# Splitting the first key load, loading one sketch matrix through GpSimd, and a new issue order in a polysketch attention and rational feed-forward kernel

## The chip, the cores and the metric

The kernel runs on one core of a Trainium2 chip. The metric is the device time of one execution in microseconds (us); lower is better.

## The reference

Linear attention with a polynomial sketch, then a feed-forward layer with a rational activation. Four batches, four heads, 1088 positions, head size 32; 4352 tokens of width 128 and a hidden width of 2048 in the second part.

```
def phi(x):                       # S1, S2: 8 x 32
    a = einsum('rd,bhsd->bhsr', S1, x)
    b = einsum('rd,bhsd->bhsr', S2, x)
    return einsum('bhsi,bhsj->bhsij', a, b)      # 64 features
q_p, k_p = phi(q), phi(k)
kv  = einsum('bhsf,bhsd->bhfd', k_p, v);  z = sum(k_p, axis=2)
num = einsum('bhsf,bhfd->bhsd', q_p, kv); den = einsum('bhsf,bhf->bhs', q_p, z) + 1e-6
x   = (num / den) as 4352 x 128
h   = x @ w_in                                    # 128 x 2048
P   = a0 + a1 h + a2 h^2 + a3 h^3
Q   = 1 + |b0| |h| + |b1| h^2
out = (P / (Q + 1e-6)) @ w_out                    # 2048 x 128
```

## The kernel before, in words

The kernel is one list of steps (976 before the change). Each step belongs to one engine and issues one or a few instructions. The schedule is written out: the table `PLACE` gives each step its position, and `run` emits the steps in that order, so every engine and every DMA queue works strictly in the order of the table. A step that has to wait holds back all that stands behind it on its engine. `ON_ACT` lists which of the steps that could run on either ScalarE (ACT) or VectorE (DVE) go to ACT. `FILLS` puts idle matmuls on TensorE (PE) in front of some places, which keep that engine running at the start. The numbers in `step` and `dma` calls (cost, rate, slack, early, land) are those of the planner that made the table; they put nothing into the program.

The work has two parts that are interleaved:

- **Attention.** `keys` handles one batch's keys: DVE transposes the key tile in 32x32 blocks into `kT` (L415, L417), PE multiplies with the sketch matrix S12 (L435), ACT copies one half of the sketches out of PSUM (`b_sk`, L440), DVE multiplies the halves to features (`k_p`, L443), PE multiplies features and values (L454), ACT keeps the result (`kvz`, L471). For the first batch ("wide") this goes in five parts. `queries` does the same for queries: transposes (L496), sketches (L518 in the "direct" form, L546 in the "spread" form, which sends the sketches through DRAM and back with DMAs), features (L530, L533, L554), products with `kvz` (L586), a division on DVE (guard L595, inverse L599, quotient L602), a transpose back on PE (L608) and a copy into `xT` on ACT (L615).
- **Feed-forward.** 29 units of up to 3072 columns each: hidden matmuls on PE (L688), evacuation on ACT (L692), |h| on DVE (L703), the denominator (L708 or L710, L713), 1/Q as exp(-ln Q) on ACT (L716, L719), polynomial products on DVE (L728, L731, L734, L746, L749), output matmuls on PE (L784), a transpose on DVE (L796) and the store. `w_in` is loaded in two halves of 1024 columns; `w_out` is loaded in two halves (called wo0 and wo1 here) and made into five scaled bf16 copies, ten steps of 128x1024 (y0f0 to y4f1; L391, L393 on ACT, L395 on DVE).

At the start nothing can be computed until data is in. S1 and S2 (1 KB each) go to the two halves of one small tile `s_raw`; DVE copies it to `s_rep` (L352, its first instruction), PE transposes that with the identity `ident` made by GpSimd (L349), and DVE makes the sketch matrices S12 and SAB from it (L355, L362). Batch 0's keys (`k0`, 128 x 4352 bytes) are loaded by ACT's DMA queue; S1, S2, the first 256 columns of the queries (`q0_a`), the values (two DMAs), the rest of the queries (`q0_b`), and the weights come by SP's queue. All DMA issues are ordinary waiting instructions of their queue.

Of the kernel before, what the change touches and what calls it, by code (L numbers as in the profile page):

```python
# [20 lines left out]
def kernel(  # L21
# [103 lines left out]
    def d_four(n, ptr):  # L125
# [88 lines left out]
    )  # L214
    ON_ACT = (
        24, 26, 28, 29, 31, 32, 328, 351, 379, 454, 478, 502, 535, 612, 636, 669, 688, 693, 744, 878, 889,
        914, 932, 946, 951, 953, 960,
    )
    FILLS = {5: 15, 14: 4, 66: 5, 70: 1}
# [46 lines left out]
    def dma(out_, in_, rank, mbytes, after=(), uses=(), eng=SP, early=0.0, rate=300, cost=0.46, slack=0.3, behind=None):  # L266
        def go():
            (nc.sync if eng == SP else nc.scalar).dma_start(out=out_() if callable(out_) else out_,
                                                            in_=in_() if callable(in_) else in_)
        return step(eng, cost, go, rank, after=after, uses=uses, land=mbytes * 1e3 / rate, early=early,  # L270
                    slack=slack, behind=behind)
# [19 lines left out]
    s_l.append(load_s(1, -205.9, SP, behind=s_l[0]))  # L291
    FIRST = 256
    k0_l = load_k(0, k0, -207, slack=0.0, rate=304, eng=ACTE)
    table = step(ACTE, 1.3, lambda: nc.scalar.preload_act_table_set("natural_log_exp_and_others"), -205, behind=k0_l[0])
    q0_a = dma(lambda: q0.t[:, 0:FIRST], flat(q, 0)[:, 0:FIRST], -203.8, 0.131, (), [q0], rate=250, slack=0.1, behind=s_l[1])
    v0_l = load_v(0, v0, -203.7, slack=0.25, rates=(180, 200), behind=q0_a)
    ab_in = []
    for c, w, x in ((4, 2, moe_b), (0, 4, moe_a)):
        ab_in.append(dma(ab_row[:, c:c + w], bass.AP(tensor=x.tensor, offset=x.offset, ap=[[w, 1], [1, w]]), -203.6, 0.001,
                         eng=ACTE, cost=0.45, slack=1.0, behind=ab_in[0] if ab_in else k0_l[0]))  # L300
    w_l = [None] * 2

    def load_w(x, rank):
        c = x * 1024
        w_l[x] = dma(w_in_sb[:, c:c + 1024], moe_w_in[:, c:c + 1024], rank, 0.524, early=LATER, rate=300, slack=0.4, behind=v0_l[1])

    load_w(0, -196)
    q0_b = dma(lambda: q0.t[:, FIRST:S], flat(q, 0)[:, FIRST:S], Q0B_RANK, 0.426, (), [q0], rate=200, slack=0.3, behind=q0_a)
    load_w(1, W1_RANK)
    k1 = Buf("kq")  # L310
    k1_l = load_k(1, k1, K1L_RANK, early=LATER, slack=0.2, behind=v0_l[1], rate=350)
# [551 lines left out]
```

## Time and profile before

| what | value |
|---|---|
| time, median of 3 runs | 266.96 us (266.92 to 267.07) |
| time of the profiled execution | 267.34 us |
| its span in the profile | 265.5 us (1.84 us lie around it) |
| granted TensorE clock, mean | 0.996 |
| DVE waits for `s_raw` before its first instruction | 4.5 us |
| data moved by DMA | 20.13 MB, mean 76 GB/s |

The profile has times from the start of the span. "Idle before" is time in which an engine stood still in front of an instruction, with what released it. SPq is SP's DMA queue. Because each engine keeps its order, a row that starts later moves all rows behind it on its engine, unless there is idle time to take it up.

### The profile page before, as it was taken

How to read it: one execution, taken by the hardware profiler on the slowest of the kernel's cores; microseconds unless marked ns; L12 is line 12 of the kernel's file. 1: busy time of each engine (PE TensorE's matmuls, PEld its weight loads, DVE VectorE, ACT ScalarE, POOL GpSimd, SP SyncE). 2: the span in 40 equal slices, each digit the busy share in tenths (PEclk: the TensorE clock that was granted, in tenths of full speed). 3: DMA queues.
4: the chain of work that ended last, by engine and by line, in shares of the span. 5: the costliest groups of instructions: out<-in, count | busy, mean ns of one | idle time of the engine just before them, and what ended most of it. 6: DMA issues, size and time to landing. Idle time of an engine off the chain costs nothing.

```text
span 265.5 us, 4239 instructions
## 1 busy us (share of the span) xinstructions
PE 257.2 (97%) x1663; PEld 140.4 (53%) x1663; DVE 252.7 (95%) x293; ACT 248.4 (94%) x209; POOL 2.7 (1%) x25
## 2 busy tenths in 40 slices
PE   7999999999999999999999999999999999999994
PEld 5767645644544464344445555444444476565682
DVE  3989899999999999999999999999999999999994
ACT  2499999999999999999999999999999999999991
POOL 4000000000000000000000000000000000000000
PEclk9999999999999999999999999999999999999998
DMA  7948344620556503035001522200002002010032
GB/s 202 331 151 223 121 127 118 159 61 0 145 131 168 164 2 108 13 79 131 28 6 44 150 65 46 41 0 0 0 10 32 0 0 40 4 29 11 0 52 40
DMA packets 29063, 20.13 MB, mean 76 GB/s; under 512 B 19316, under 2 KB 24948, under 8 KB 29044
## 3 DMA queue, kind: packets, MB, share of 16 engines
q1 hardware_dynamic: 28352, 19.24, 28.8%
q10 hardware_dynamic: 692, 0.62, 0.8%
q8 instruction: 13, 0.21, 0.4%
q14 instruction: 6, 0.05, 0.1%
HBM read 16.65 MB, written 3.21 MB: 75 GB/s over the span
## 4 chain that ended last, share of the span: by engine, by line
PE 35%; ACT 29%; DVE 21%; issue 8%; DMA 4%; SPq 1%; DVEq 0%; ACTq 0%
PE h_ps L688 21%; ACT t L692 7%; ACT ln L716 7%; ACT t L719 7%; PE out_ps L784 6%; ACT t L725 5%; DVE t L713 4%; DVE t L728 4%; DVE t L731 3%; DMA kq<-in_q_dram 3%; DVE t L749 2%; PE att_ps L586 2%; DVE t L703 2%; PE att_ps L546 2%; DVE t L708 2%
## 5 line engine op out<-in xcount | busy, mean ns | idle before, releaser
L688 PE MATMUL h_ps<-xT,w_in_sb 128*128 128x512 f32 (+1 forms) x320 | 128.0, 535 | 0.8 <-ACT xT L615 0.6
L784 PE MATMUL out_ps<-t,w_out 128*128 128x512 bf16 (+1 forms) x498 | 101.7, 346 | 0.6 <-DVE t L728 0.5
L688 PEld LDWEIGHTS h_ps<-xT,w_in_sb 128*128 128x128 f32 x320 | 58.6, 190 | 45.2 <-issue 33.8
L784 PEld LDWEIGHTS <-w_out 128*128 128x128 bf16 x498 | 47.4, 98 | 51.9 <-issue 21.1
L692 ACT CAST t<-h_ps 128x1024 bf16<-128x1024 f32 (+1 forms) x69 | 68.5, 1025 | 0.9 <-PE h_ps L688 0.9
L716 ACT ACTIVATE ln<-t 128x3072 f32<-128x3072 bf16 (+4 forms) x29 | 64.7, 2230 | 0.3 <-DVE t L713 0.2
L719 ACT ACTIVATE t<-ln 128x3072 bf16<-128x3072 f32 (+4 forms) x29 | 64.7, 2232 | 0.1
L713 DVE TENSOR_TENSOR t<-t,t 128x3072 bf16<-128x3072 bf16 (+4 forms) x29 | 40.4, 1392 | 0.6 <-ACT t L710 0.6
L728 DVE TENSOR_TENSOR t<-t,t 128x3072 bf16<-128x3072 bf16 (+4 forms) x29 | 40.4, 1394 | 0.0
L731 DVE TENSOR_TENSOR t<-t,t 128x3072 bf16<-128x3072 bf16 (+3 forms) x23 | 32.6, 1423 | 0.1
L725 ACT ACTIVATE t<-t,a_sb 128x3072 bf16<-128x3072 bf16 (+2 forms) x12 | 32.0, 2665 | 0.0
L703 DVE TENSOR_SCALAR t<-t 128x3072 uint16<-128x3072 uint16 (+4 forms) x29 | 22.5, 776 | 0.3 <-ACT t L692 0.2
L734 DVE TENSOR_TENSOR t<-t,t 128x3072 bf16<-128x3072 bf16 (+1 forms) x13 | 21.6, 1660 | 0.0
L708 DVE TENSOR_SCALAR t<-t,b_abs 128x3072 bf16<-128x3072 bf16 (+2 forms) x22 | 21.5, 975 | 0.1
L586 PEld LDWEIGHTS att_ps<-kvz,a_all 128*64 128x64 f32 x288 | 9.6, 137 | 6.8 <-issue 2.2
L586 PE MATMUL att_ps<-kvz,a_all 128*64 128x66 f32 x288 | 11.5, 226 | 0.6 <-DVE a_all L530 0.4
L749 DVE TENSOR_TENSOR t<-t,t 128x1024 bf16<-128x1024 bf16 (+3 forms) x10 | 11.2, 1124 | 0.1
L710 ACT ACTIVATE t<-t,b_abs 128x1024 bf16<-128x1024 bf16 (+4 forms) x7 | 11.3, 1611 | 0.0
L554 DVE TENSOR_TENSOR a_all<-a_all,b_all 128x768 f32<-128x768 f32 (+2 forms) x11 | 9.6, 869 | 0.0
L443 DVE TENSOR_TENSOR k_p<-att_ps,b_sk 128x768 f32<-128x768 f32 x9 | 8.4, 949 | 0.8 <-ACT b_sk L440 0.6
L454 PEld LDWEIGHTS att_ps<-v_sb,k_p 128*64 128x64 f32 x216 | 6.7, 138 | 2.3 <-issue 1.3
L746 DVE TENSOR_TENSOR t<-t,t 128x3072 bf16<-128x3072 bf16 (+3 forms) x6 | 7.7, 1276 | 0.0
(74 smaller groups left out, 143.8 us busy)
## 6 DMA issues: line engine op xcount, KB each, us to landing
a_all<-sk_d SPq DMA_DIRECT2D x6, 384.0 KB, 3.9
b_all<-sk_d SPq DMA_DIRECT2D x12, 192.0 KB
kq<-in_k_dram SPq DMA_DIRECT2D x3, 544.0 KB, 7.3
kq<-in_q_dram SPq DMA_DIRECT2D x3, 544.0 KB
a_all<-sk_d SPq DMA_DIRECT2D x4, 320.0 KB
b_all<-sk_d SPq DMA_DIRECT2D x8, 160.0 KB
v_sb<-in_v_dram SPq DMA_DIRECT2D x4, 288.0 KB, 4.9
v_sb<-in_v_dram SPq DMA_DIRECT2D x4, 256.0 KB, 4.3
```

The costliest lines, as they stand in the source:

```text
L586: nc.tensor.matmul(nd.t[x:x + 64, o:o + 2 * KW], lhsT=(av(c)[:, o0 + x:o0 + x + 64] if how == "direct" else q_p.t[:, c * n + o0 + x:c * n ...
L688: nc.tensor.matmul(h.t[:, cols[x] - cols[x0]:cols[x + 1] - cols[x0]], lhsT=w_in_sb[:, f * 128:(f + 1) * 128], rhs=xT[:, xpos(t0):xpos(t0) ...
L692: nc.scalar.copy(out=hh.t[:, cols[x0]:cols[x1]], in_=h.t[:, 0:cols[x1] - cols[x0]])
L703: nc.vector.tensor_scalar(out=u.t[:, :n].bitcast(U16), in0=hh.t[:, :n].bitcast(U16), scalar1=0x7FFF, scalar2=None, op0=AX.bitwise_and)
L708: nc.vector.tensor_scalar(out=w.t[:, :n], in0=u.t[:, :n], scalar1=ab1, scalar2=ab0, op0=AX.mult, op1=AX.add)
L713: nc.vector.tensor_mul(out=y.t[:, :n], in0=w.t[:, :n], in1=u.t[:, :n])
L716: nc.scalar.activation(out=ln.t[:, :n], in_=y.t[:, :n], func=ACT.Ln, bias=1.0 + 1e-6)
L719: nc.scalar.activation(out=r.t[:, :n], in_=ln.t[:, :n], func=ACT.Exp, scale=-1.0)
L725: nc.scalar.activation(out=p.t[:, :n], in_=hh.t[:, :n], func=ACT.Identity, scale=a3, bias=a2)
L728: nc.vector.tensor_mul(out=s.t[:, :n], in0=hh.t[:, :n], in1=r.t[:, :n])
L731: nc.vector.tensor_mul(out=(hh if mode == 3 else p).t[:, :n], in0=hh.t[:, :n], in1=s.t[:, :n])
L784: nc.tensor.matmul(o[0].t[:, :bl[x][1]], lhsT=w_sb[y_][:, bl[x][2], :], rhs=src.t[:, cols[x]:cols[x + 1]], start=(o[1] == 1), stop=(o[1] = ...
```

## The change

- Batch 0's keys are loaded in two DMAs, both on ACT's queue, one behind the other: the first half of the columns (2176 bytes of each of 128 partitions), then the second. The DVE transposes of the wide keys are cut to match: instead of two pieces that both read the whole tile (tiles 0 to 4, tiles 4 to 8 with the rest), there are three: tiles 0 to 8 of the first half (one instruction of 128x512), then tiles 0 to 4 and tiles 4 to 8 with the rest of the second half. The first sketches of keys wait for the first two pieces.
- S2 is loaded by a DMA of GpSimd, the first thing that GpSimd does in the kernel's body, ahead of its memsets. SP no longer issues S2.
- The memset of the tile `idle`, which the idle matmuls read, moves from GpSimd to DVE.
- `PLACE`, `FILLS` and the planner's numbers are new; the order of nearly all 978 steps is different. `ON_ACT` is the same for all units; of the ten `w_out` steps, y1f1 and y3f0 go from DVE to ACT and y0f0 and y1f0 from ACT to DVE.

The new table gives these orders at the start (the place of a step decides; K is the first batch's keys, p0 to p4 its five parts, Q1 the queries 0 to 256, Q2 256 to 512, Q3 512 to 768, Q4 the rest):

```
DVE before: s_rep, K tiles 0-4, S12, Q1 transpose, SAB x2, p0 features, K tiles 4-8 + rest, p1, p3, p2, Q1 features, p4,
            Q3/Q2/Q4 transposes, y4f1, Q1 guard/inverse/quotient, Q2 features, y1f1, Q2 division, y3f0, y0f1, next keys, unit 0
DVE after:  s_rep, K first half, S12, K second half 0-4, 4-8 + rest, SAB x2, Q1 transpose, p0, p1, p3, p2, Q1 features, p4,
            Q3/Q2/Q4 transposes, y0f1, Q1 guard/inverse/quotient, Q2 features, y1f0, Q2 division, next keys, y0f0, unit 0
ACT before: k0, moe_b, moe_a, table, p0, b_abs, a_sb, p1, p3, Q1, p2, p4 copies, kvz, Q3 copy, y2f1, Q2 copy, y3f1, Q1 xT,
            y2f0, y0f0, y1f0, unit 0 evacuation
ACT after:  k0 first, k0 second, moe_b, moe_a, table, p0, a_sb, p2, p1, b_abs, p3, Q1, p4 copies, y3f1, y2f1, kvz, Q3 copy,
            y3f0, Q2 copy, Q4 copy, Q1 xT, y1f1, y4f0, unit 0 evacuation
SP before:  S1, S2, q0_a, v0 low, v0 high, q0_b, wo1, wo0, w_in first half, next keys, ...
SP after:   S1, q0_a, v0 low, v0 high, wo1, q0_b, wo0, w_in first half, next keys, ...
```

The diff, with the tables cut:

```
 PLACE = (
-    0, 3, 1, 19, 6, 7, 8, 2, 18, 16, 9, 58, 55, 12, 10, 4, 5, 13, 24, 25, 49, 21, 23, 22, 83, 97, 84,
...
+    0, 1, 3, 4, 8, 9, 10, 11, 5, 6, 24, 16, 96, 25, 23, 12, 2, 13, 14, 20, 21, 15, 28, 29, 34, 108, 63,
...
-    24, 26, 28, 29, 31, 32, 328, ...
+    28, 29, 30, 31, 32, 33, 330, ...
-FILLS = {5: 15, 14: 4, 66: 5, 70: 1}
+FILLS = {13: 12, 18: 3, 74: 1, 79: 1}
...
-s_l.append(load_s(1, -205.9, SP, behind=s_l[0]))
+nc.gpsimd.dma_start(out=s_raw[R:2 * R], in_=S2)
+def go():
+    pass
+s_l.append(step(POOL, 0.65, go, -205.9, land=0.003, early=0.75, slack=0.4))
-k0_l = load_k(0, k0, -207, slack=0.0, rate=304, eng=ACTE)
+k0_l = []
+for m in range(2):
+    x = slice(m * S // 2, (m + 1) * S // 2)
+    k0_l.append(dma(lambda x=x: k0.t[:, x], flat(k, 0)[:, x], -207 + 0.1 * m, 0.279, (), [k0], rate=(460, 380)[m], slack=0.15,
+                    eng=ACTE, behind=k0_l[0] if m else None, name=("first", "go")[m]))
...
-nc.gpsimd.memset(idle, 0.0)
+nc.vector.memset(idle, 0.0)
...
+            if m is not None:
+                nc.vector.transpose(out=hT[:, m, :, t0:t1], in_=halves(kb.t, t0, t1)[:, m])
...
-    pieces = ((0, 4, (0, 1), False), (4, 8, (0, 1), True)) if wide else ((0, 8, (0,), False), (0, 8, (1,), True))
+    if wide:
+        pieces = ((0, 8, (), False, 0), (0, 4, (), False, 1), (4, 8, (), True, 1))
+        costs, loads = (0.6, 0.33, 0.33 + 0.15), (k_l[:1], k_l, k_l)
+    else:
+        pieces = ((0, 8, (0,), False), (0, 8, (1,), True))
...
-        sk = step(PE, 0.13 * n + 0.1, sketches, r - 0.2, after=(tr[:1] if wide and t1 <= 4 else tr) + s12, uses=[kT, ab],
+        sk = step(PE, 0.13 * n + 0.1, sketches, r - 0.2, after=(tr[:2] if wide and t1 <= 4 else tr) + s12, uses=[kT, ab],
```

More of the change, by code (lines that the diff above doesn't have):

```diff
@@ L165 @@
     PLACE = (
[48 rows of a table removed]
[48 rows of a table added]
     )
     ON_ACT = (
-        24, 26, 28, 29, 31, 32, 328, 351, 379, 454, 478, 502, 535, 612, 636, 669, 688, 693, 744, 878, 889,
-        914, 932, 946, 951, 953, 960,
+        28, 29, 30, 31, 32, 33, 330, 353, 381, 456, 480, 504, 537, 614, 638, 671, 690, 695, 746, 880, 891,
+        916, 934, 948, 953, 955, 962,
     )
-    FILLS = {5: 15, 14: 4, 66: 5, 70: 1}
+    FILLS = {13: 12, 18: 3, 74: 1, 79: 1}
     NW = 5 if '4' in MODES else 3
@@ L264, with dma @@
     k0, q0, v0 = Buf("kq"), Buf("kq"), Buf("v_sb")
-    def dma(out_, in_, rank, mbytes, after=(), uses=(), eng=SP, early=0.0, rate=300, cost=0.46, slack=0.3, behind=None):
+    def dma(out_, in_, rank, mbytes, after=(), uses=(), eng=SP, early=0.0, rate=300, cost=0.46, slack=0.3, behind=None, name="go"):
         def go():
@@ L269, in go @@
                                                             in_=in_() if callable(in_) else in_)
+        go.__name__ = name
         return step(eng, cost, go, rank, after=after, uses=uses, land=mbytes * 1e3 / rate, early=early,
@@ L290 @@
     s_l = [load_s(0, -206, SP)]
-    s_l.append(load_s(1, -205.9, SP, behind=s_l[0]))
+    nc.gpsimd.dma_start(out=s_raw[R:2 * R], in_=S2)
+    def go():
+        pass
+    s_l.append(step(POOL, 0.65, go, -205.9, land=0.003, early=0.75, slack=0.4))
     FIRST = 256
-    k0_l = load_k(0, k0, -207, slack=0.0, rate=304, eng=ACTE)
-    table = step(ACTE, 1.3, lambda: nc.scalar.preload_act_table_set("natural_log_exp_and_others"), -205, behind=k0_l[0])
-    q0_a = dma(lambda: q0.t[:, 0:FIRST], flat(q, 0)[:, 0:FIRST], -203.8, 0.131, (), [q0], rate=250, slack=0.1, behind=s_l[1])
-    v0_l = load_v(0, v0, -203.7, slack=0.25, rates=(180, 200), behind=q0_a)
+    k0_l = []
[3 more added lines that the diff above has]
+                        eng=ACTE, behind=k0_l[0] if m else None, name=("first", "go")[m]))
+    table = step(ACTE, 1.3, lambda: nc.scalar.preload_act_table_set("natural_log_exp_and_others"), -205, behind=k0_l[1])
+    q0_a = dma(lambda: q0.t[:, 0:FIRST], flat(q, 0)[:, 0:FIRST], -203.8, 0.131, (), [q0], rate=350, slack=0.2, behind=s_l[0])
+    v0_l = load_v(0, v0, -203.7, slack=0.4, rates=(340, 205), behind=q0_a)
     ab_in = []
@@ L299 @@
         ab_in.append(dma(ab_row[:, c:c + w], bass.AP(tensor=x.tensor, offset=x.offset, ap=[[w, 1], [1, w]]), -203.6, 0.001,
-                         eng=ACTE, cost=0.45, slack=1.0, behind=ab_in[0] if ab_in else k0_l[0]))
+                         eng=ACTE, cost=0.45, slack=1.0, behind=ab_in[0] if ab_in else k0_l[1]))
     w_l = [None] * 2
@@ L304, in load_w @@
         c = x * 1024
-        w_l[x] = dma(w_in_sb[:, c:c + 1024], moe_w_in[:, c:c + 1024], rank, 0.524, early=LATER, rate=300, slack=0.4, behind=v0_l[1])
+        w_l[x] = dma(w_in_sb[:, c:c + 1024], moe_w_in[:, c:c + 1024], rank, 0.524, early=LATER, rate=430, slack=0.4, behind=v0_l[1])
     load_w(0, -196)
-    q0_b = dma(lambda: q0.t[:, FIRST:S], flat(q, 0)[:, FIRST:S], Q0B_RANK, 0.426, (), [q0], rate=200, slack=0.3, behind=q0_a)
+    q0_b = dma(lambda: q0.t[:, FIRST:S], flat(q, 0)[:, FIRST:S], Q0B_RANK, 0.426, (), [q0], rate=330, slack=0.4, behind=q0_a)
     load_w(1, W1_RANK)
     k1 = Buf("kq")
-    k1_l = load_k(1, k1, K1L_RANK, early=LATER, slack=0.2, behind=v0_l[1], rate=350)
+    k1_l = load_k(1, k1, K1L_RANK, early=LATER, slack=1.3, behind=v0_l[1], rate=390)
     wo_l = [dma(lambda f0=f0: w_raw.t.rearrange("p (f d) -> p f d", d=d_model)[:, f0:f0 + nf // 2],
                 moe_w_out.rearrange("(fo fi) d -> fi fo d", fi=128)[:, f0:f0 + nf // 2], WO_RANK, 0.525, (), [w_raw],
-                early=LATER, rate=310, slack=0.4, behind=v0_l[1]) for f0 in (0, nf // 2)]
+                early=LATER, rate=318, slack=0.4, behind=v0_l[1]) for f0 in (0, nf // 2)]
     idle = consts.tile([128, 256], BF, name="idle")
-    nc.gpsimd.memset(idle, 0.0)
+    nc.vector.memset(idle, 0.0)
     nc.gpsimd.memset(ones, 1.0)
@@ L369 @@
     st = step(DVE, 0.15, mk_rep, -210, after=s_l)
-    st = step(PE, 0.11, mk_st, -202, after=[st], uses=[s_ps], early=2.7)
+    st = step(PE, 0.11, mk_st, -202, after=[st], uses=[s_ps], early=2.0)
     s12 = [step(DVE, 0.15, mk_s12, -200, after=[st], uses=[s_ps])]
@@ L410, in keys, with transposes @@
         kv = Buf("out" if wide else "att")
-        def transposes(t0, t1, us, rest):
+        def transposes(t0, t1, us, rest, m=None):
             hT = kT.t[:, 0:HALF].rearrange("p (t u g m) -> p m u t g", u=2, m=2, g=32)
+            if m is not None:
+                nc.vector.transpose(out=hT[:, m, :, t0:t1], in_=halves(kb.t, t0, t1)[:, m])
             for u in us:
@@ L418, in transposes @@
                                     in_=kb.t.rearrange("p (m x) -> p m x", m=2)[:, :, HALF // 2:])
-        pieces = ((0, 4, (0, 1), False), (4, 8, (0, 1), True)) if wide else ((0, 8, (0,), False), (0, 8, (1,), True))
-        tr = [step(DVE, 0.6 + 0.07 * wide + 0.15 * pc[3], lambda pc=pc: transposes(*pc), rank - 0.3, after=k_l, uses=[kb, kT],
-                   early=early) for pc in pieces]
+        if wide:
[3 more added lines that the diff above has]
+            pieces = ((0, 8, (0,), False), (0, 8, (1,), True))
+            costs, loads = (0.6, 0.6 + 0.15), (k_l, k_l)
+        tr = []
+        for pc, c, ld in zip(pieces, costs, loads):
+            turn = lambda pc=pc: transposes(*pc)
+            turn.__name__ = "first" if pc[-1] == 0 and wide else "<lambda>"
+            tr.append(step(DVE, c, turn, rank - 0.3, after=ld, uses=[kb, kT], early=early))
         last = None
@@ L562, in queries @@
                        lambda j=j: c.t[j * 2 * half:(j + 1) * 2 * half, :n2],
-                       rank, n2 * 256e-6, [st], [c, d], rate=260, slack=GAP) for j in range(2)]
+                       rank, n2 * 256e-6, [st], [c, d], rate=200, slack=GAP) for j in range(2)]
             puts[-1] = put[-1]
@@ L566, in queries @@
                        lambda: bass.AP(tensor=d.t.tensor, offset=d.t.offset, ap=[[2 * QN, 2 * R], [0, R], [1, 2 * n]]),
-                       rank, n * 1.024e-3, put, [d, a], rate=230, cost=0.57, slack=GET_SLACK)]
+                       rank, n * 1.024e-3, put, [d, a], rate=230, cost=0.57, slack=GET_SLACK - 0.2)]
             for h2 in range(2):
@@ L571, in queries @@
                                                      ap=[[0, R], [2 * QN, R], [1, 2 * n]]),
-                               rank, n * 0.512e-3, put, [d, bb], rate=85, cost=0.6, slack=GET_SLACK, behind=get[-1]))
+                               rank, n * 0.512e-3, put, [d, bb], rate=95, cost=0.6, slack=GET_SLACK, behind=get[-1]))
             ft = step(DVE, d_one(2 * n), features, rank, after=get, uses=[a, bb])
```

94 rows, old and new, of the table PLACE are left out of this document.

## The prediction

> **What bounds the kernel now.** First the page's busy times, then busy time by stretches, then the waits of the stretch in the middle.
>
> ```profile
> PE 257.2 (97%) x1663; PEld 140.4 (53%) x1663; DVE 252.7 (95%) x293; ACT 248.4 (94%) x209; POOL 2.7 (1%) x25
> ```
> ```profile
> core 0: us, PE busy (x) PEld busy (x) DVE busy (x) ACT busy (x) POOL busy (x), PEclk, DMA share, GB/s
> 8.00:17.00 9.00, 8.05 (x143) 6.27 (x138) 7.60 (x22) 6.18 (x14) 0.00 (x0) 1.00 0.98 291
> 17.00:34.00 17.00, 16.44 (x184) 11.44 (x183) 15.86 (x31) 15.84 (x23) 0.00 (x0) 1.00 0.50 146
> 34.00:245.00 211.00, 209.68 (x1163) 105.42 (x1160) 209.08 (x205) 209.65 (x154) 0.00 (x0) 1.00 0.25 60
> ```
>
> Three engines are full together. From 34 to 245 us DVE stands still for 211.00 - 209.08 = 1.9 us and ACT for 1.35, so there is little to win there by any order. The change neither adds nor removes work of weight: `ON_ACT` sends the same unit steps to ACT. So only idle time can be won, and it lies at the start: DVE idles 4.5 us in front of its first instruction, 1.4 from 8 to 17 and 1.1 from 17 to 34; ACT idles 2.8 and 1.2 in the same two stretches. The chain of waits and the timeline say why.
>
> ```profile
> 1.19 3.22 DMA s_raw<-in_S_dram
> 4.50 0.23 DVE s_rep L352
> ```
> ```profile
> 4.37 0.36 SPq L268 DMA_DIRECT2D kq<-in_q_dram  x1
> 4.50 0.21 DVE L352 COPY s_rep<-s_raw 16x128 f32<-16x128 f32 x1 [4.50 <-DMA s_raw<-in_S_dram]
> 4.65 0.75 DVE L415 STREAM_TRANSPOSE kT<-kq 128x256 f32<-128x256 f32 x2
> 10.57 0.76 DVE L496 STREAM_TRANSPOSE qT<-kq 128x256 f32<-128x256 f32 x2
> 11.26 0.43 ACT L471 COPY kvz<-out_ps 64x66 f32<-64x66 f32 x2 [1.70 <-PE out_ps L454]
> 15.05 0.36 ACT L615 COPY xT<-att_ps 128x256 f32<-128x256 f32 x1
> ```
>
> One kilobyte of S2, issued at 1.19, lands 3.22 us later and releases everything. The view of DMA from 1.7 to 3.2 us has the reason: ACT's queue (q10, the keys) moved 102 packets, SP's queue (q1) 9. S2 stood behind all of k0 on the DMA engines. k0 itself was in by 4.37: the issue of `q0_b` at 4.37 waits for its semaphore. From 4.50 to 10.57 DVE runs almost without a gap.
>
> **S2 by GpSimd.** No row shows a DMA of GpSimd. It can be issued at 0.73, where GpSimd's memset of `idle` starts now. Lower bound for landing: SP's first bytes move at 1.7 in the view of DMA, so hardly before 2.1. Upper bound: S2's 4.41 of today (rival c goes past it). Nearest is today's S2 with half of k0 ahead of it: bytes start at 1.7 and k0 takes until 4.37, half of that is 1.3, which gives 3.0, and 0.4 from the last byte to the wait (k0's last packets fall before 4.0 in the view of DMA) gives 3.4. I take 3.4; a gain of 1.1 us in this one wait. The Trainium skill (DMA: Bandwidth & Descriptors, "Anatomy of one DMA") puts the fixed cost of a GpSimd DMA at about 2.0 us; by it S2 would land near 2.75 if nothing were in the way, an estimate that no row here tests. GpSimd's later memsets move by the issue, bounded by 0.28 us (SP's issue of S2) and 0.75 (SP's longest issue by then): `ident`, ready at 1.7 and needed by PE behind `s_rep`, covers 2 us of it. `idle` on DVE costs between 0 and 0.4 us (a 128x256 DVE instruction takes 0.41) inside DVE's first wait: nothing. The 13 idle matmuls now ahead of PE's first transpose take 13 x 0.21 (16 took 3.3 us), until about 3.7, near where `s_rep` lets PE go on.
>
> The Trainium skill (SBUF — State Buffer, "SBUF: two separate sides", the box on DVE blocking a DMA) speaks against this edit: while DVE runs certain fast copies, GpSimd cannot write descriptors. Here DVE does nothing but the small memset before `s_rep`, so by that rule S2 would lose at most that memset's 0.4 us and land at 3.8, which moves the sum by under 0.1 us, since the keys decide (next); no row here shows the effect.
>
> **Keys in two halves.** First half: in by about 3.3 (as above). Second: not before 4.37, since the bytes are the same, and `q0_a`, issued 0.33 earlier now, may be served between the halves: 0.13 MB at the 231 to 300 GB/s of these stretches is 0.5 us, so at most 4.9; I take 4.65. DVE: `s_rep` 3.4, first half 0.68 (the 128x512 transposes of the next keys), S12, done at 4.3; then a wait for the second half until 4.65 (0.35 us, new). So the second half, not S2, sets the start unless S2 is later than 3.75. Behind it: 0.35 + 0.5 (two transposes and the rest, by starts), SAB 0.4, Q1 transpose 0.35, p0 features 0.34, at 6.6. p1 waits on PE and ACT: tiles 4-8 done 5.5, sketches of p2 and p1 0.9, copy 0.25, so 6.77 (0.17 of waiting). From p1 to Q3's transpose today: 10.57 - 7.32 = 3.25. So Q3's transpose starts at 10.0, against 10.57: **0.55 us won** (0.25 to 0.95 with the bounds of the second half).
>
> **`q0_b` behind wo1.** Q3's transpose needs `q0_b`, whose issue now stands behind 0.52 MB of wo1. Ahead of its last byte are k0 0.56, `q0_a` 0.13, v0 0.56, wo1 0.52, itself 0.43: 2.20 MB. The view of DMA up to 9.5 us shows 2.22 MB moved, so it lands at 9.45 + 0.4 = 9.85. Cover 0.15 us; each us later costs a us. wo0 (2.72 MB; 2.81 MB had moved by 11.4) is in by 11.7, w_in's first half (3.25 MB; 3.35 by 12.8) by 13.
>
> **ACT's new order.** y3f1 and y2f1 (1.15 + 1.05) go into the 1.70 us of idle time ahead of `kvz`. From 9.0 they end at 11.2, so `kvz` starts at 11.2 instead of 11.26: the 0.55 us are lost to it there, but 1.7 us of ACT's idle time is filled. Then Q3 copy to 11.9, y3f0 to 13.05, Q2 copy and Q4 copy to 13.9, Q1's `xT` copy at 13.9 (today 15.05; its division on DVE ends by 13.2). Q2 features come 0.5 earlier, its products end at 15.0, unit 0's hidden matmuls take 2 us, and unit 0's evacuation starts at 17.0 (today 18.34). About 1.3 us won on ACT. DVE carries 0.74 less of `w_out` before unit 0 and pays it back right behind.
>
> **The sum.** DVE wins 0.55, and up to 1.5 of its 2.5 us of later idle time (8 to 34 us) if ACT's lead of 1.3 reaches it; both engines are full afterwards, so the smaller lead counts: between 0.55 and 1.3, I take 1.0. The middle is a new order at 1.9 us of idle time; I put 0.2 us of loss on it. Net -0.8: 267.34 of the profiled execution becomes 266.5, and from the median, which is 0.38 below that execution, 266.96 - 0.8 = **266.2 us**. The tail is unchanged: the last unit's chain has the same steps in the same order.
>
> **Rivals.**
> (a) *The transfers come no earlier.* Halves and a third queue share the same DMA engines; S2 lands near 4.4 as now and the second half near 4.9. By the walk above with `s_rep` at 4.5, Q3's transpose starts within 0.1 us of 10.57. Left is what ACT's order gives, 0 to 0.5: 266.5 to 267.0, no change that counts. For: the 102 to 9 packets. Against: GpSimd can issue at 0.73, S2 was issued at 1.19. The rule of the Trainium skill (DMA: Bandwidth & Descriptors, "Issuing engines are not separate DMA queues") says that more issuers save issue time only; the packets agree with it as far as they go. Chance 0.19.
> (b) *The new order opens bubbles in the middle.* Place: 34 to 245 us, where an in-order engine meets a step before its input. With today's durations summed in the two orders, unit 9's `d_s` (L728) moves ahead of 8 us of DVE work and its ln (L716) ahead of 10 us of ACT work, among the largest moves. A step that is one 3072-column evacuation early (1.0 us) costs that much on all three engines. Two of them, less the 1.0 won, with the 1.9 idle of today kept: 266.96 - 1.0 + 2.0 = 268.0. It decides once idle time of DVE there rises from 1.9 past 1.9 + 1.0 + 0.5. For: the order of today is tight there, a new one can hardly be tighter. Against: unit totals are the same, and unit 9's `d_s` moves less than the ln and exp that it waits for. Chance 0.24.
> (c) *S2 through GpSimd is late.* If its issue and landing take over 3.8 us (from 0.73), DVE, PE and ACT all start later, one for one; at 5.5 the time is 267.0 + 1.0 - 0.4 = 267.6. Nothing shows a price that high. Chance 0.06.
> (d) *All idle time of 8 to 34 us goes too:* 0.95 + 1.0, 265.0 to 265.5. Chance 0.1.
>
> **How the numbers follow.** A measurement of this kernel can tell 0.2%, 0.53 us, from no change. The forecast has 0.41 with 265.8 to 266.4; with (d), faster is 0.51. (a) gives same 0.19. (b) and (c) give slower 0.30. The range leaves out the lower end of (d) and about half of (b): 265.3 to 267.9.
>
> **What would show it.** `s_rep` at 3.0 to 3.8; the second transpose piece waiting on the key DMA at about 4.3 to 4.7; Q3's transpose at 9.7 to 10.3 without a DMA wait; `kvz` near 11.2 behind two `w_out` steps; unit 0's evacuation near 17; DVE idle from 34 to 245 us within 1.5 to 2.5. Wrong: `s_rep` after 4.3, a wait on `q0_b` at 10, or more than 3.4 us idle in the middle.

## The result: 0.9% slower, and the profile after

The changed kernel takes **269.43 us** (median of 4 runs, 268.95 to 269.67) against 267.0 for before (median of 4), a ratio of 1.009 with a 95% interval of 1.0076 to 1.0104. Its profiled execution took 269.61 us with a span of 267.8, 2.3 us more than before's 265.5. Ten more executions of the same kernel (after_again, below) gave 269.56 (268.03 to 271.62). The forecast was 266.2, faster; it was wrong in sign.

The page's busy times, then busy time by stretches, show at once that no work was added and that the middle is not where the time went.

```profile
PE 257.4 (96%) x1637; PEld 141.5 (53%) x1655; DVE 252.6 (94%) x293; ACT 248.7 (93%) x209; POOL 3.1 (1%) x25
```
```profile
core 0: us, PE busy (x) PEld busy (x) DVE busy (x) ACT busy (x) POOL busy (x), PEclk, DMA share, GB/s
8.00:17.00 9.00, 8.98 (x136) 6.14 (x134) 6.07 (x14) 5.63 (x15) 0.00 (x0) 1.00 0.77 248
17.00:34.00 17.00, 15.44 (x188) 12.04 (x187) 15.37 (x35) 14.99 (x23) 0.00 (x0) 1.00 0.86 175
34.00:245.00 211.00, 208.66 (x1145) 105.25 (x1162) 209.49 (x209) 209.40 (x154) 0.00 (x0) 1.00 0.25 60
```

From 34 to 245 us DVE idles 211.00 - 209.49 = 1.51 us, less than before's 1.92. From 8 to 17 us it now idles 2.93 (1.40 before), and PE is busy for 8.98 of 9.00 us (8.05 before) with fewer matmuls (136 against 143; a few records are missing): **TensorE, which had slack at the start, has become the bound there, by slower matmuls.** Unit 0's evacuation, ACT's first step of the feed-forward part, starts at 20.36 instead of 18.34, which is 2.0 of the 2.3 us; from there to the end it is 247.4 us against 247.2. Before, then after:

```profile
18.34 1.00 ACT L692 CAST t<-h_ps 128x1024 bf16<-128x1024 f32 x1
20.36 1.01 ACT L712 CAST t<-h_ps 128x1024 bf16<-128x1024 f32 x1 [0.81 <-PE h_ps L708]
```

The chain of waits and the timelines of DVE and PE:

```profile
1.23 3.53 DMA s_raw<-in_S_dram
4.79 0.23 DVE s_rep L362
```
```profile
4.79 0.21 DVE L362 COPY s_rep<-s_raw 16x128 f32<-16x128 f32 x1 [3.79 <-DMA s_raw<-in_S_dram]
8.73 0.96 DVE L463 TENSOR_TENSOR k_p<-h_ps,b_sk 128x768 f32<-128x768 f32 x1 [1.16 <-ACT b_sk L460]
10.48 0.69 DVE L463 TENSOR_TENSOR k_p<-h_ps,b_sk 128x512 f32<-128x512 f32 x1 [0.80 <-ACT b_sk L460]
13.22 0.76 DVE L516 STREAM_TRANSPOSE qT<-kq 128x256 f32<-128x256 f32 x2
```
```profile
1.25 2.77 PE L331 MATMUL att_ps<-idle 128*128 128x256 bf16 x12
5.15 0.25 PE L359 MATMUL att_ps<-ident,s_rep 16*128 16x16 f32 x1 [1.14 <-DVE s_rep L362]
8.34 1.23 PE L538 MATMUL att_ps<-qT,SAB 64*128 64x256 f32 x4
10.55 1.23 PE L538 MATMUL att_ps<-qT,SAB 64*128 64x256 f32 x4
```

S2 lands at 4.77 us, not 3.4, later than before's 4.41. The idle matmuls end at 4.02 and PE then waits 1.14 us, where before waited 0.44. And four query matmuls of 256 columns take 1.23 us; before, eight of them took 1.13. PE's timeline before:

```profile
1.29 3.14 PE L321 MATMUL att_ps<-idle 128*128 128x256 bf16 x15
4.87 0.20 PE L349 MATMUL att_ps<-ident,s_rep 16*128 16x16 f32 x1 [0.44 <-DVE s_rep L352]
5.00 0.61 PE L321 MATMUL out_ps<-idle 128*128 128x256 bf16 x4
6.49 1.13 PE L518 MATMUL att_ps<-qT,SAB 64*128 64x256 f32 x8
```

That is TensorE's clock. The clock column shows 1.00 here because the trace has an event only where the clock changes; by those events full clock is granted at 4.02 us before and at **11.95 us** after. Until then PE runs at half speed (the event at the end of the span gives 0.5), ACT's copies of sketches wait for PE, and DVE's features wait for ACT (the 1.16 and 0.80 above).

The traces also show when it is granted. Full clock lasts 259.41 us in before (76 x 3.413) and 256.00 in after (75 x 3.413), and a whole number of 3.413 us in every kept trace: the clock changes only at the ends of stretches of that length, which begin at another place in each execution. For the profiled executions of several kernels, named below, the next table gives PE's busy share in stretches around the start, the share that was idle matmuls, and the columns that the stretch's matmuls moved (256 for an idle one, 64 for a small f32 one; each matmul shared out over the time until the next one starts; to tens):

| kernel | stretch, us | PE busy | idle matmuls | columns | full clock at its end |
|---|---|---|---|---|---|
| before | 0.60 to 4.02 | 0.86 | 0.86 | 3550 | yes |
| e3 | 0.38 to 3.79 | 0.80 | 0.80 | 3210 | yes |
| e1 | 2.45 to 5.87 | 0.98 | 0.93 | 3530 | yes |
| e9 | 2.76 to 6.17 | 0.99 | 0.68 | 3330 | yes |
| after | 1.71 to 5.12 | 0.67 | 0.67 | 2520 | no |
| after | 5.12 to 8.53 | 0.99 | 0.24 | 2670 | no |
| after | 8.53 to 11.95 | 1.00 | 0 | 2980 | yes |
| e6 | 2.55 to 5.96 | 0.62 | 0.62 | 2280 | no |
| e11, first run | 2.43 to 5.84 | 0.88 | 0.70 | 2690 | no |
| e11, first run | 5.84 to 9.26 | 1.00 | 0 | 2910 | no |
| e4 | 4.53 to 7.95 | 0.21 | 0.08 | 540 | no, lost |
| e4 | 7.95 to 11.36 | 1.00 | 0 | 3190 | yes |

A gap of 1.1 us is enough to miss one stretch, and after's next one misses too although PE shows as busy. Busy share doesn't settle it: 1.00 went both ways. The count of columns does: in all 37 stretches around the starts of the 15 kept traces, full clock followed none of those with up to 2922 columns and each of those with 2978 or more. That is read from traces with a few records missing, the margin is thin, and no run was made to test it.

The Trainium skill (TensorE: Matmul & The Clock Gate, "Part 1: The HAM clock gate") states the free-running window of 3413 ns, and the trace agrees to the third digit. The same part of the Trainium skill puts the ramp's penalty under 1% of a typical kernel span and advises against fitting a specific count of cold matmuls. Here that rule is at its edge: the executions of after alone differ by more than 1% (268.03 to 271.62), and most of the 0.9% lost is the late clock, as e1 shows.

Since the stretches run free, each execution meets the start at another phase. So the times of one kernel spread: 93 of 97 executions of before that ran beside the kernels below lie between 266.5 and 268.0 us, four near 270, and after spreads over 3.6 us. A median of few executions depends on which phases it met.

### The profile page after: what moved, and what is told of

The parts are those of the page before. It is cut to its first block, busy times and chain, and to the rows that moved or that the text cites. A ratio compares the mean times of both kernels' runs of the same rounds, so it can differ in the third digit from the quotient of the medians.

```text
span 267.8 us, 4205 instructions
## 1 busy us (share of the span) xinstructions
PE 257.4 (96%) x1637; PEld 141.5 (53%) x1655; DVE 252.6 (94%) x293; ACT 248.7 (93%) x209; POOL 3.1 (1%) x25
## 4 chain that ended last, share of the span: by engine, by line
ACT 41%; PE 28%; DVE 15%; issue 9%; DMA 5%; SPq 1%; DVEq 0%; ACTq 0%; POOLq 0%
PE h_ps L708 14%; ACT ln L736 12%; ACT t L739 11%; ACT t L712 9%; PE out_ps L804 6%; ACT t L745 6%; DVE t L748 3%; DVE t L733 3%; DMA b_all<-sk_d 3%; DVE t L769 2%; PE att_ps L606 2%; DVE t L751 1%; DMA s_raw<-in_S_dram 1%; PE att_ps L566 1%; DVE t L723 1%
## 5 line engine op out<-in xcount | busy, mean ns | idle before, releaser
L804 PE MATMUL out_ps<-t,w_out 128*128 128x512 bf16 (+1 forms) x480 | 98.7, 345 | 1.5 <-issue 0.6
L712 ACT CAST t<-h_ps 128x1024 bf16<-128x1024 f32 (+2 forms) x69 | 69.8, 1046 | 1.5 <-PE h_ps L708 1.5
L751 DVE TENSOR_TENSOR t<-t,t 128x3072 bf16<-128x3072 bf16 (+3 forms) x23 | 32.8, 1429 | 0.1
L745 ACT ACTIVATE t<-t,a_sb 128x3072 bf16<-128x3072 bf16 (+2 forms) x12 | 32.3, 2690 | 0.0
L730 ACT ACTIVATE t<-t,b_abs 128x1024 bf16<-128x1024 bf16 (+4 forms) x7 | 11.2, 1620 | 0.0
L474 PE MATMUL att_ps<-v_sb,k_p 128*64 128x64 f32 x216 | 7.8, 225 | 0.1
```

Source lines behind the costliest of these rows:

```text
L712: nc.scalar.copy(out=hh.t[:, cols[x0]:cols[x1]], in_=h.t[:, 0:cols[x1] - cols[x0]])
L745: nc.scalar.activation(out=p.t[:, :n], in_=hh.t[:, :n], func=ACT.Identity, scale=a3, bias=a2)
L751: nc.vector.tensor_mul(out=(hh if mode == 3 else p).t[:, :n], in0=hh.t[:, :n], in1=s.t[:, :n])
L804: nc.tensor.matmul(o[0].t[:, :bl[x][1]], lhsT=w_sb[y_][:, bl[x][2], :], rhs=src.t[:, cols[x]:cols[x + 1]], start=(o[1] == 1), stop=(o[1] = ...
```

## The experiments

after_again is the kernel after, unchanged, over more executions:

> The changed kernel itself once more, for more executions. Theory 1 now reads: TensorE goes to full clock only at the end of a stretch of 3.41 us in which it was busy for more than some 70 to 80%, and where these stretches begin differs from execution to execution. The gap from 4.0 to 5.15 spoils every stretch but those that end between about 3.7 and 4.9. So about two thirds of the executions at 269 to 269.7, one third near 267. Theory 2 (S2 is late, at a fixed price): all within 0.3 us of 269.4.

Measured: 269.56 us (268.03 to 271.62, 10), ratio 1.0084 (1.0047 to 1.0121). No execution is below 268.03, so the loss does not hang on a few unlucky phases. Theory 1 as worded above put a third of the executions near 267; none came, so its count of phases was too kind. Theory 2 missed too: the spread is 3.6 us, not 0.6.

The expectations number their theories as follows, and write "Theory 1" for T1. **Theory T1:** the loss is TensorE's late clock, brought on by the gap between the idle matmuls and `s_rep`, and that gap comes from S2 through GpSimd. **Rivals:** T2, the later S2 costs one for one and the new order the rest; T3, the new order itself (ACT's and the loads') loses. A fourth theory is explained where it is tried, under the order of the loads.

### The clock

e1: the kernel after with five more idle matmuls, so that PE has no gap before `s_rep`. S2 stays as late as it is.

```
-    FILLS = {13: 12, 18: 3, 74: 1, 79: 1}
+    FILLS = {13: 17, 18: 3, 74: 1, 79: 1}
```

> The changed kernel with 17 instead of 12 idle matmuls ahead of TensorE's first transpose, nothing else. Theory 1 (cold TensorE: the 13 idle matmuls end at 4.0 us, TensorE then stands still for 1.1 us and runs its matmuls at half speed until 11.95): the matmuls of 5 to 12 us take about 0.22 us again instead of 0.31, the transpose of the queries 512 to 768 starts near 11 instead of 13.2, time 267.0 to 267.6. Theory 2 (S2 through GpSimd is late and each us costs one): only 0.3 us is at stake in that, so 269.1 to 269.5. Theory 3 (the new order costs it further on): 269.0 to 269.5.

Measured: 267.59 us (266.59 to 269.47, 10 executions), ratio to before 1.0026 (0.9991 to 1.0061). The profiled execution took 267.41, 2.2 less than after's; the medians of ten differ by 2.0. PE's, DVE's and ACT's timelines of e1:

```profile
5.16 0.25 PE L359 MATMUL att_ps<-ident,s_rep 16*128 16x16 f32 x1
8.71 0.70 PE L538 MATMUL att_ps<-qT,SAB 64*128 64x256 f32 x4
```
```profile
4.80 0.21 DVE L362 COPY s_rep<-s_raw 16x128 f32<-16x128 f32 x1 [3.79 <-DMA s_raw<-in_S_dram]
11.04 0.76 DVE L516 STREAM_TRANSPOSE qT<-kq 128x256 f32<-128x256 f32 x2
```
```profile
18.09 1.01 ACT L712 CAST t<-h_ps 128x1024 bf16<-128x1024 f32 x1 [0.80 <-PE h_ps L708]
```

S2 is as late as in after (4.80), but full clock comes at 5.87, four query matmuls take 0.70 instead of 1.23, Q3's transpose starts at 11.04 instead of 13.22 and the first evacuation at 18.09 instead of 20.36. So some 2 us hang on the clock alone, as T1 had put (267.0 to 267.6); T2 falls.

e2: the other side, the kernel before with three idle matmuls fewer.

```
-FILLS = {5: 15, 14: 4, 66: 5, 70: 1}
+FILLS = {5: 12, 14: 4, 66: 5, 70: 1}
```

> The kernel before with 12 instead of 15 idle matmuls ahead of the first transpose, so 13 in all as in the changed kernel. Theory 1: TensorE stands still from about 3.9 to 4.9 us, runs slow for some 6 to 7 us, time 268.8 to 269.6. Theories 2 and 3: 266.9 to 267.1, no change.

Measured: 267.75 (266.76 to 269.88, 10), ratio 1.002 (0.9976 to 1.0065). The interval says nothing, the executions do: five lie at 266.8 to 266.9, as T2 and T3 put, and five at 268.6 to 269.9, about as T1 put, two groups that differ by 2 to 3 us. In the profiled one (266.94) S2 was in at 4.15 and the stretch to 5.32 was 0.86 busy. That the slower five missed a stretch is argued, since none of them has a trace; before with its 15 idle matmuls is near 270 in only 4 of 97 executions.

### S2's way

e3: the kernel after with S2 on SP's queue behind S1, as before. e6: the kernel before with S2 by GpSimd and the `idle` memset on DVE.

```
e3, against after:
-nc.gpsimd.dma_start(out=s_raw[R:2 * R], in_=S2)
...
+s_l.append(load_s(1, -205.9, SP, behind=s_l[0]))
e6, against before:
-s_l.append(load_s(1, -205.9, SP, behind=s_l[0]))
+nc.gpsimd.dma_start(out=s_raw[R:2 * R], in_=S2)
...
-nc.gpsimd.memset(idle, 0.0)
+nc.vector.memset(idle, 0.0)
```

> The changed kernel with S2 issued by SP right behind S1 again, still 12 idle matmuls. Theory 1: if S2 lands near 3.4 to 3.8, TensorE's gap shrinks to a few tenths and the slow stretch may go: 266.5 to 267.3; if it lands at 4.4 as in the kernel before, the gap is still 0.7 us and the time 268.8 to 269.4. Theory 2: 0.3 us faster than the changed kernel, 269.1. Theory 3: 269.1 to 269.5.

> The kernel before with S2 issued by GpSimd first and the memset of the idle tile on VectorE, as in the change, but with the order and the 15 idle matmuls of before, and the keys in one load. Theory 1: S2 lands at 4.7 to 4.8 instead of 4.4, the 16 idle matmuls end at 4.4, TensorE stays fast: 267.2 to 267.4, the price of S2 alone. Theory 2: the same 0.3 us, or more if each engine behind it loses more: 267.2 to 268. Theory 3: no forecast beyond that.

Measured: e3 267.23 (265.96 to 269.29, 10), ratio 0.9996 (0.9954 to 1.0037); e6 270.24 (268.04 to 270.4, 10), ratio 1.0087 (1.0055 to 1.0119). DVE's first wait in each, e3 first:

```profile
3.67 0.21 DVE L357 COPY s_rep<-s_raw 16x128 f32<-16x128 f32 x1 [2.67 <-DMA s_raw<-in_S_dram]
10.86 0.76 DVE L511 STREAM_TRANSPOSE qT<-kq 128x256 f32<-128x256 f32 x2
```
```profile
5.82 0.22 DVE L357 COPY s_rep<-s_raw 16x128 f32<-16x128 f32 x1 [4.81 <-DMA s_raw<-in_S_dram]
```

S2 through GpSimd alone puts the whole loss on the kernel before (full clock at 12.79), and taking it out of the kernel after removes the loss; T3 falls with it, as far as e3's interval reaches. e3 came out as T1 put. No theory put e6 right: the highest forecast was 268, because S2 was expected at 4.7 to 4.8 and was waited for until 5.82, so that even with 15 idle matmuls PE waited 1.53 us for it. On SP's queue S2 gets through at 3.67, between the halves of the keys: the split does what it was for, and S2 needed no third queue. e3's median is before's, but its executions run from 265.96 to 269.29, and the profiled one is the fastest, with a span of 264.1 against 265.5. Of these 1.4 us only 0.3 are won ahead of the first evacuation (18.01 against 18.34); the rest comes behind it (under the order of the loads). Q3's transpose is at 10.86 even with full clock at 3.79, among other things because PE waits for the values:

```profile
8.34 0.45 PE L469 MATMUL out_ps<-v_sb,k_p 128*64 128x64 f32 x8 [0.93 <-DMA v_sb<-in_v_dram]
```

The trace has the reason: the issue of the values' second half starts at 3.60 instead of 2.72, on the semaphore of the first key load; two loads in place of one have moved which load it waits for.

e9: the kernel before with the keys in two DMAs (one step, all else as it was, 12 idle matmuls as in e2).

```
-    FILLS = {5: 15, 14: 4, 66: 5, 70: 1}
+    FILLS = {5: 12, 14: 4, 66: 5, 70: 1}
...
-    k0_l = load_k(0, k0, -207, slack=0.0, rate=304, eng=ACTE)
+    def load_k0():
+        for m in range(2):
+            x = slice(m * S // 2, (m + 1) * S // 2)
+            nc.scalar.dma_start(out=k0.t[:, x], in_=flat(k, 0)[:, x])
+
+    k0_l = [step(ACTE, 0.92, load_k0, -207, uses=[k0])]
```

> The kernel before with nothing changed but the keys in two loads, issued together, all transposes waiting for both as before, and 12 instead of 15 idle matmuls, since S2 should come earlier. If the split is what lets S2 of SP's queue through, VectorE starts at 3.6 to 3.9 instead of 4.5, its first transposes at 4.4 to 4.7 with the second half: the queries 512 to 768 are transposed at 10.2 to 10.5 (10.57 before). Theory 1: median 266.5 to 267.2 with TensorE's gap closed. If the split does nothing for S2: VectorE starts at 4.2 to 4.5, and the time is that of the kernel before with 12 idle matmuls, 267.7.

Measured: 267.6 (266.8 to 269.89, 10), ratio 1.0017 (0.9982 to 1.0052). `s_rep` starts at 3.71, with none of the new order: the split alone brings S2 0.8 us forward. Q3's transpose came at 10.96, not at 10.2 to 10.5, and the median missed its forecast: before's DVE order waits for the whole tile, and the values' second half is issued late here too (3.56).

e4: S2 first on ACT's queue, ahead of both key loads.

```
-nc.gpsimd.dma_start(out=s_raw[R:2 * R], in_=S2)
...
+s_l.append(load_s(1, -205.9, ACTE, behind=s_l[0]))
```

> The changed kernel with S2 issued by ACT ahead of the two halves of the keys, 12 idle matmuls. S2 then lands near 2.2 to 2.6 and VectorE begins at about 2.5, or at the landing of the first half. Theory 1: TensorE's gap before the first transpose is gone, but the second half of the keys comes 0.4 us later (4.9), so TensorE's next gap grows to 0.7: median 267 to 268. Theory 2 (S2 sets the time, one for one): 265.5 to 266.5.

Measured: 269.72 (268.87 to 270.91, 10), ratio 1.0089 (1.0062 to 1.0116): the earliest S2 of all, and as slow as after; both forecasts missed (267 to 268, 265.5 to 266.5). DVE's timeline:

```profile
2.27 0.72 DVE L357 COPY s_rep<-s_raw 16x128 f32<-16x128 f32 x1 [1.28 <-DMA s_raw<-in_S_dram]
4.19 0.71 DVE L420 STREAM_TRANSPOSE kT<-kq 128x512 f32<-128x512 f32 x1 [1.20 <-DMA kq<-in_k_dram]
7.01 0.77 DVE L420 STREAM_TRANSPOSE kT<-kq 128x256 f32<-128x256 f32 x2 [2.00 <-DMA kq<-in_k_dram]
```

The second half of the keys is issued a little later and now shares the DMA engines with `q0_a` and the values: its last packets move at 6.4 us, in e3 at 4.1. PE stands without work for 2.69 us; full clock comes at 4.53, is lost at 7.95 and comes back at 11.36. One load moved by one place delays another by some 2.5 us (7.01 against e3's 4.55).

e5: e3 with three more idle matmuls behind S2's transpose (`18: 3` becomes `18: 6`).

> The changed kernel with S2 issued by SP behind S1, and 6 instead of 3 idle matmuls ahead of the first sketches, to close TensorE's gap of 0.35 us there. Theory 1: fewer late clocks than with S2 on SP and 3 idle matmuls, median 266.3 to 267.0, best 266.0. Theory 2 and 3: as with 3 idle matmuls, median 267.2.

Measured: 267.64 (266.15 to 269.04, 10), ratio 1.0007 (0.9972 to 1.0042): no gain, and T1's forecast missed; five of the ten still take 268.0 to 269.0.

### Why S2 is late through GpSimd

Its issue starts at 1.23, not 0.73, takes 0.64, and its first data packet moves at 3.72 (SP's S1: issue 0.74, packets 1.69). DVE's memset of `idle` can't have held it back: it runs from 0.84 to 1.01, ahead of the issue. Either GpSimd's path is slow by itself (P) or S2 waits behind the keys (Q). e10 put ACT's table load ahead of the key loads, to delay them.

```
+    nc.scalar.preload_act_table_set("natural_log_exp_and_others")
     FIRST = 256
     k0_l = []
...
```

> The changed kernel with ACT's table load ahead of the two key loads, which are so issued 1.3 us later; S2 by GpSimd as in the change. It asks why S2 lands only at 4.8 to 5.4. Theory Q (S2's packets stand behind those of the keys on the DMA engines): with the keys out of the way S2 lands near 3.0 to 3.4 and VectorE's first instruction starts there. Theory P (a DMA of GpSimd takes that long by itself): S2 lands at 4.7 to 5.4 as before, although nothing big stands in its way. The time itself gets worse, since the keys come later.

Measured, in one execution: 269.59 us; S2's first packet at 3.74. The keys were still issued at 0.77 and 1.18, so the table load held nothing back and nothing is told. e13 holds all bulk loads with real dependencies: `k0_go` issues the first key load, and `q0_a` on SP's queue has to wait for the second copy.

```
+    def hold():
+        nc.scalar.copy(out=k0.t[0:2 * R, 0:D], in_=s_raw)
+        nc.scalar.copy(out=q0.t[0:2 * R, 0:D], in_=s_raw)
+        k0_go()
...
+    k0_go, k0_l[0].fn = k0_l[0].fn, hold
...
```

> The kernel after, with all bulk loads held until S2 is in: two small ScalarE copies of s_raw into the key and query tiles stand ahead of the key loads, so the keys (ScalarE's queue) and the first queries and values (SyncE's queue) cannot start before S1 and S2 have landed. S2 is still the first thing that GpSimd issues. Only S1 shares the DMA engines with it. Theory P (GpSimd's path is slow by itself): S2's first packet still comes near 3.7 us, 3.70 to 3.84 in the five kernels so far that load it this way, and s_rep starts at 4.2 or later. Theory Q (S2 waits behind the keys on the DMA engines, as in the kernel before): its first packet comes about 1 us after its issue of 1.2 to 1.9, so at 2.2 to 2.9, and s_rep starts by 3.2. Between 3.2 and 4.2 both share it. The time itself is no measure, since all of the keys come later: about 2.5 us more than the kernel after by P, about 1 us more by Q.

Measured, in one execution: 272.24 us, with all loads late. GpSimd's and DVE's timelines:

```profile
1.24 0.64 POOL L292 DMA_DIRECT2D s_raw<-in_S_dram  x1 [0.79 <-POOLq L875]
```
```profile
3.07 0.21 DVE L370 COPY s_rep<-s_raw 16x128 f32<-16x128 f32 x1 [2.07 <-DMA s_raw<-in_S_dram]
```

The issue is the same, but the first data packet moves at 2.56 and `s_rep` starts at 3.07: Q holds. Of S2's 4.77 us in after, 1.7 are due to the bulk loads; whether S2 stood behind them or was slowed by them, e13 doesn't part. The order of issue fits the first. When S2's first packet moved in after, `q0_a` and 0.44 of the keys' 0.56 MB had moved: GpSimd's issue takes from 1.23 to 1.87 and ends behind that of the second half (1.16 to 1.64), where SP's in e3 takes from 1.19 to 1.47. From the issue, 1.24, to the wait's end it takes 1.8 us with free engines. The 2.0 us that the Trainium skill (DMA: Bandwidth & Descriptors, "Anatomy of one DMA") gives as the fixed cost of a GpSimd DMA is near that; the 1.7 us that decided here come on top.

### The order of the loads

In after, the first spread queries' reads (`b_all`) stand behind the second half of `w_in` and the next values on SP's queue, and DVE waits for them:

```profile
27.85 0.69 DVE L574 TENSOR_TENSOR a_all<-a_all,b_all 128x512 f32<-128x512 f32 x1 [1.04 <-DMA b_all<-sk_d]
```

e1 has this wait as well (1.23 us), and so has e5, which is e3 but for three idle matmuls:

```profile
25.70 0.69 DVE L569 TENSOR_TENSOR a_all<-a_all,b_all 128x512 f32<-128x512 f32 x1 [1.16 <-DMA b_all<-sk_d]
```

e3's profiled execution, the earliest, doesn't have it (24.39). Theory 4 is that this wait costs what it shows. e11 is e3 with the next values' first half behind those reads; e12 is e11 with `w_in`'s second half also earlier.

```
e11: steps[117].place = 102.5                    e12: and steps[12].place = 25.5
```

> The changed kernel with S2 by SP (12 and 3 idle matmuls), and the first half of the next batch's values issued behind the three reads of the first spread queries (a_all, b_all) instead of ahead of them. The reads then stand behind one transfer less, 256 KB, about 1 us. Theory 4 (apart from the start, the new order loses 1.2 to 1.4 us where VectorE waits for b_all near 27 us, in all executions but the earliest): VectorE's wait is gone or under 0.4 us, the rest from the first evacuation on takes 246.1 us as in the best execution, median 266.2 to 266.8. If the wait is of no weight for the end: 267.2.

> As the kernel with the later values, and the second half of w_in issued right behind the next keys (8.5 us) instead of behind the writes of the first spread queries (14 to 16 us). The reads of a_all and b_all then have no large transfer ahead. Theory 4: no wait for b_all, median 266.0 to 266.6, faster than the kernel before. Against it: the writes of the spread sketches queue behind w_in and land 1 to 2 us later, which gives part of it back.

> The same kernel as e11_v1_later, for more executions. If its gain came from the loads' order (next values behind the reads of the spread queries), the median stays at 266.2 to 266.6 and the ratio below 0.998. If it came from the phase of the clock in the eight executions of that run (six of them had an early one), the median moves toward that of e3_s2_sp, 267.0 to 267.3, with the ratio at 0.999 to 1.002; the executions with a boundary between 3.6 and 4.8 us would still be near 266.1 and those past 5.5 at 268 to 269.

Measured: e11 266.25 (265.99 to 268.09, 8), ratio **0.9964** (0.9951 to 0.9977); the same kernel again 266.69 (265.81 to 269.04, 12), ratio **0.9994** (0.9971 to 1.0016); e12 267.0 (266.04 to 268.4, 12), ratio 1.0002 (0.9984 to 1.0021), above its forecast of 266.0 to 266.6. The wait on `b_all` is gone in both executions of e11 that were profiled, also in the first, whose evacuation comes at 20.17, nearly as late as after's (first run, then the second):

```profile
26.54 0.68 DVE L570 TENSOR_TENSOR a_all<-a_all,b_all 128x512 f32<-128x512 f32 x1
24.63 0.68 DVE L570 TENSOR_TENSOR a_all<-a_all,b_all 128x512 f32<-128x512 f32 x1
```

From the first evacuation to the end, the profiled executions with the wait take 247.4 to 247.6 us (after, e1, e5), those without it 246.1 to 246.2 (e3, e11 twice, e12), and before 247.2. So the wait costs some 1.3 us, and without it the new order is 1.1 us faster than before's in this part.

The second run's median lies between its two forecasts, and its ratio where the phase was to put it: it took back most of the first one's gain. Where the clock goes down at the end of an execution gives the phase, and from it the end of the first stretch that the idle matmuls can fill (to about 0.5 us where the fall lies inside the span). By that, e11's 20 executions and the 97 of before:

| stretch ends at | before, median (n) | e11, median (n) |
|---|---|---|
| 3.6 to 4.6 us | 266.74 (21) | 266.10 (5) |
| 4.6 to 5.6 us | 266.85 (23) | 266.27 (8) |
| 5.6 to 7.0 us | 267.20 (53) | 268.09 (7) |

The first row is sound: the fall is seen in all its executions, and e11 is 0.6 us faster there. In the other two rows the fall is seen in 6 of e11's 15 executions and 16 of before's 76; for the rest the end of the span stands in for it, so they are in part sorted by the very time that is compared. What can be said is that the four executions of e11 whose late phase is seen took 268.09 to 269.04. In the one of them with a trace, the stretch from 5.84 to 9.26 was busy all through, with 2910 columns, and did not bring full clock. So the change without GpSimd's DMA, and with the reads ahead of the values, is a little faster where the clock comes early; over all phases a gain isn't shown.

## Why the prediction was wrong, step by step

- **S2 by GpSimd, 3.4 us: failed.** It landed at 4.77, past the upper bound of 4.41. The lower bound of 2.1 was not reached even with free engines (3.07 in e13). The step that failed is "half of k0 ahead of it": the issue came 0.5 later than put and took 0.64, and 0.44 of k0's 0.56 MB and all of `q0_a` moved first. The issue at 0.73, taken from where the memset started, was not GpSimd's to have: GpSimd's own queue releases its DMA at 1.23 only (in e13's row, `[0.79 <-POOLq L875]` at 1.24).
- **The idle matmuls, "until about 3.7, near where `s_rep` lets PE go on": the missing term.** They ended at 4.02 and `s_rep` let PE go on at 5.15. The sum had no price for a gap on PE, though `FILLS` was in the diff with three idle matmuls fewer ahead of `s_rep`. The gap cost 2.2 us by e1's profiled execution. This is the step that turned the sign. The rows were there: before's PE already waits 0.44 us for `s_rep`, and its idle matmuls start 0.21 us apart until 4 us and 0.12 apart from 5 us on.
- **Rival (c), S2 late, came about**: issue and landing took 4.04 us from 0.73, past its 3.8. Its price, one for one, was the error: by its own sum an S2 that late gives 267.0 + 0.3 - 0.4 = 266.9, no change. e6 shows the real price, 3 us for 1.3 us of delay, because the late clock comes with it.
- **Keys in two halves: right, with no gain to show.** The second half was in by 4.55 in e3 (4.65 put) with no wait, and "unless S2 is later than 3.75" is the case that happened. From `s_rep` to p0's features after took 2.40 us, the walk 2.5 without its wait.
- **Q3's transpose at 10.0: failed twice.** 13.22 with the slow clock; still 10.86 in e3, where p1 starts at 6.71 (6.77 put) but the 3.25 us behind it became 4.15: the values come later, among other things, and the walk took that stretch over from before unchanged.
- **`q0_b` behind wo1: not refuted.** Q3's transpose waits for no DMA, but at 10.86 (e3) and 13.22 it comes later than the 10.0 for which the cover of 0.15 us was put.
- **ACT's order: half right.** The two `w_out` steps stand ahead of `kvz` as put, but they end at 14.4 (12.05 in e3), not 11.2, since ACT's copies before them follow PE. The first evacuation came at 18.01 in e3 against 17.0 put and 18.34 before: 0.3 of the 1.3 us.
- **The middle: the number right by luck.** 0.2 us of loss put, 0.2 measured from the first evacuation to the end. But from 34 to 245 us nothing was lost: DVE idles 1.51 there against 1.92 before, and rival (b) did not come about. The 0.2 is the difference of two things that no step had priced: the wait on `b_all` near 27 us (1.3 us) and a new order that is 1.1 us faster without it (e3, e11).
- **Rival (a)** had the packets right: S2 landed behind the keys. No change that counts, its outcome, is e3's, where S2 came at 3.67: for another reason.

The sum put -0.8. Measured by the profiled executions: +2.2 from the late clock, and little from everything else together, since e1, which has all of the change but the gap, can't be told from before. That little is made of parts that cancel: the wait on `b_all` against the gains of the new order.

## What to carry to other kernels

Where TensorE idles at the start, treat the idle matmuls as a bridge that must reach the first real dense matmuls, with a margin for every load behind it: here a gap of one microsecond kept TensorE at half clock for seven more (5.12 to 11.95). A small load that releases everything should be issued first on a queue that issues early, and a bulk load split so that the small one goes between; here another issuing engine did not bring it past the loads already issued. Take such a start over many executions, and look at the clock's phase where the trace shows it, before believing 0.3%.

## What was not expected of the hardware

- PE shown as busy for 0.99 or 1.00 of a stretch did not always bring full clock (after, 5.12 to 8.53; e11, 5.84 to 9.26), while 0.80 of idle matmuls of 256 columns did (e3). What parts the stretches of these traces is the number of columns moved, somewhere between 2922 and 2978 in 3.413 us; a run that tests it is open.
- Full clock is lost again after one stretch with too little work (e4: 0.21 busy, lost at 7.95 us).
- ACT's table load does not hold back DMA issues behind it on ACT's queue (e10: 0.77 and 1.18 us); copies that wait do (e13: 3.70 us).
